# Memory's key rows turned on VectorE and put in place through DRAM, in an attention and gated-FFN kernel

## The chip, the cores and the metric

One Trainium2 chip, one of its cores. The metric is the device time of one execution in microseconds (us). Matmuls run on TensorE (PE in the profile; PEld is its loading of the stationary operand), elementwise work on VectorE (DVE), ScalarE (ACT) and GpSimd (POOL). Transfers are issued by SyncE (SP) and GpSimd and carried out by 16 DMA engines. SBUF is the memory on the chip with 128 partitions, PSUM the eight banks into which TensorE writes, and DRAM the memory off the core.

## The reference

The layer is `x + A(xn) + B(xn)`, with `xn` the normalised `x` of 2048 tokens and D = 448 features. B is a gated FFN. A is attention in four segments of 512 tokens with a memory that is carried from segment to segment; cut to what matters here:

```python
for s in range(4):                       # segments; H = 16 heads of 28
    qs, ks, vs = q[:, :, s], k[:, :, s], v[:, :, s]
    a_dot = softmax(qs @ ks.T * scale + mask) @ vs
    pq = phi(qs)                         # phi(t) = t + 1 if t > 0 else exp(t)
    a_mem = (pq @ M) / (pq @ z + 1e-6)   # the recall
    outs.append(g * a_mem + (1 - g) * a_dot)
    pk = phi(ks)
    M = M + einsum("bhld,bhle->bhde", pk, vs)   # the update
    z = z + pk.sum(tokens)
return concat(outs) @ wo
```

The update sums over tokens, so on TensorE it needs `phi(k)` with the tokens on the partitions. The products of keys and queries have the features there. The rows of `phi(k)` therefore have to be turned.

## The kernel before

The program has two parts. In the **front** (0 to about 140 us) four blocks of 512 tokens pass one after the other; a block is a segment. After it, attention inside the segments, the FFN and the output projection run interleaved, and the change doesn't touch them.

In the front all queues but GpSimd's follow the order in which the code is written. For block `b` it is:

1. `values(b, t)` for the four token tiles t = 0 to 3: 11 matmuls into a PSUM bank `pv` (tag "p", two banks), then a copy by ScalarE into `vst` (`store_values`). After the last tile `vst` goes to DRAM. For b > 1, `recall(b-1)` stands behind tile 3: 16 matmuls of `phi` with the memory state `mst`. For block 0 the value tiles have code of their own ahead of the loop.
2. Seven products `keys_queries(b, c)`, c = 0 to 6, of 128 features each (keys are features 0 to 447, queries 448 to 895): 11 matmuls into `pp`. Even c take a bank of tag "p", odd c one of tag "gu" (two each), so value tiles 0 and 1 of the next block take the banks that products 4 and 6 had. ScalarE and VectorE read `pp` into `qk` and, where needed, into `e`, which is `phi` of the product; the last reader of a bank is VectorE's line 360. `qk` goes to DRAM (`qd`), and the query part of `e` too (`fd`); `phi_queries` reads `fd` back as `phi`, in the layout of the recall, after product 6.
3. Between the products stand: `key_rows` for key chunks 0 to 3, at k = 2 to 5 (TensorE turns four 128x128 pieces of `e` with the identity into a bank `pk`, ScalarE copies that into `kn`); `turn` of the four tiles of the next block's `xn` (`pt`, then `xs`); `normalise` of `xn` for the next block; and in blocks 2 and 3 `divide` and `answer` of the previous block's recall (VectorE's `rc`, GpSimd's scaling of `phi`, VectorE's transpose into `tb`, GpSimd's transfer to `od`).
4. After product 6, for blocks 0 to 2, `update(b)`: 64 small matmuls of `kn` with `vst` into `pmm`, which VectorE adds into `mst`.

VectorE, ScalarE, TensorE and SP each do their instructions in that order; an instruction that waits holds all behind it. SBUF tiles of one name share a fixed number of buffers (`bufs`), and a new tile waits until the one that had its buffer is no longer read.

Of the kernel before, what the change touches and what calls it, by code (L numbers as in the profile page):

```python
# [16 lines left out]
P = 128  # L17
D = 448
# [45 lines left out]
def kernel(  # L64
# [87 lines left out]
    def eight_k(dtype, name):  # L152
        return mid.tile([P, 8, 256], dtype, name=name, tag="8k")
# [128 lines left out]
    with tc.tile_pool(name="front", bufs=2) as sb, tc.manual_schedule(engines=FRONT):  # L282
# [6 lines left out]
        mst = [sb.tile([P, P], F32, name=f"mst{n}", bufs=1) for n in range(2)]  # L289
        one = sb.tile([P, 1], F32, name="one", bufs=1)  # L290
        kn = eight_k(F32, "kn").rearrange("p (t a) n -> p t (a n)", t=NT)

# [48 lines left out]
        def values(b, t):  # L341
            pv = bank("pv", "p")
            value_terms(b, t, pv, TERMS)
            store_values(b, t, pv)

        def keys_queries(b, c):
# [7 lines left out]
            if (c < 4 and b < NB - 1) or (c > 2 and b > 0):  # L354
                e = sb.tile([P, L], F32, name="e", bufs=4)
                A.activation(e, pp, AF.Relu, scale=-1.0)  # L356
                A.activation(e, e, AF.Exp, scale=-1.0)
# [12 lines left out]

        def key_rows(c, e):

            pk = bank("pk", ("m", "pd")[c % 2])
            for t in range(NT):
                T.transpose(pk[:, t * P:(t + 1) * P], e[:, t * P:(t + 1) * P], ident)  # L375
            n = min(P, D - c * P)
            A.activation(kn[:, :, c * P:c * P + n], pk.rearrange("p (t n) -> p t n", t=NT)[:, :, :n], AF.Copy)

# [36 lines left out]
        def answer(b, i, phi):  # L415
            tb = sb.tile([P, L], F32, name="e", bufs=4) if b == NB - 1 else sb.tile([P, L], F32, name="tb", bufs=2)
            V.transpose(tb, phi[:, i])
            nc.gpsimd.dma_start(od[b][P * i:P * (i + 1)], tb)
# [132 lines left out]
        for b in range(NB):  # L551
# [28 lines left out]
            for k, c in enumerate(LAST if last else range(7)):  # L580
                e[c] = keys_queries(b, c)
                if b == 0 and c + 4 < 7:
                    split_qk(c + 4)
                if b > 1:
                    i = k + (1 if last else -1)
                    if 0 < i <= NG:
                        answer(b - 1, i - 1, phi)
                    if 0 <= i < NG:
                        divide(i, phi)
# [13 lines left out]
                if last:  # L603
# [4 lines left out]
                    continue  # L608
                if 2 <= k < 6:
                    key_rows(k - 2, e[k - 2])  # L610
                if k == 6:
                    update(b)
                n = k - 1 if b == 0 else k + 1
# [282 lines left out]
```

## Time and profile before

| | us |
|---|---|
| median of 3 runs (674.81 to 675.7) | 675.15 |
| the profiled execution | 675.51 |
| its span in the profile | 673.7 |
| PE busy in the span | 668.8 |
| DVE busy | 555.1 |
| ACT busy | 341.8 |
| POOL busy | 169.1 |

The profile is of one execution. Its rows give an engine, an operation, tile names as `out<-in`, the count, the busy time and the mean of one in ns, and behind the bar the idle time ahead of them with what ended it. The chain of work that ended last goes back from the last instruction to whatever released each step; TensorE's granted clock is full over the whole span (0.999). `L360` is line 360 of the kernel.

### The profile page before, as it was taken

To read this page: it belongs to the slowest core of one execution; us is meant where nothing else is said; L and a number is where in the kernel's file an instruction comes from. 1 tells how busy PE (TensorE), PEld (TensorE's weight loads), DVE (VectorE), ACT (ScalarE), POOL (GpSimd) and SP (SyncE) were. 2 spreads that over 40 slices of the span, in tenths; PEclk is the share of its full clock that TensorE was granted. 3 is DMA by queue.
4 is the path that set the end of the run, shared out by engine and by line. 5 is a ranking of instruction groups with operands and counts; after the bars stand their busy time and mean duration, and the time that the engine had idled before them with its cause. 6 is when DMAs were issued, how large, how long until landed. Compare 5 with 4: busy or idle time off the path is not lost.

```text
span 673.7 us, 11186 instructions
## 1 busy us (share of the span) xinstructions
PE 668.8 (99%) x3963; PEld 555.5 (82%) x3963; DVE 555.1 (82%) x967; ACT 341.8 (51%) x559; POOL 169.1 (25%) x368
## 2 busy tenths in 40 slices
PE   8999999999999999999999999999999999999998
PEld 8888888878878778787887878787787878778897
DVE  6855584758998989998998899988988898989964
ACT  4947574533646446354554555554554656444320
POOL 4402051305122223122322322222231332221000
PEclk9999999999999999999999999999999999999999
DMA  8536668797123242323243324224342432315272
GB/s 273 189 149 249 226 230 274 268 305 214 41 73 89 71 137 64 102 57 103 70 104 93 85 80 102 61 70 102 88 111 72 85 73 77 65 44 134 68 216 97
DMA packets 46223, 84.42 MB, mean 125 GB/s; under 512 B 6360, under 2 KB 21080, under 8 KB 45656
## 3 DMA queue, kind: packets, MB, share of 16 engines
q1 hardware_dynamic: 43160, 76.37, 37.6%
q0 software_dynamic: 3008, 7.34, 5.3%
q8 instruction: 31, 0.51, 0.3%
q14 instruction: 24, 0.20, 0.1%
HBM read 51.05 MB, written 32.64 MB: 124 GB/s over the span
## 4 chain that ended last, share of the span: by engine, by line
PE 93%; DVE 2%; issue 1%; DMA 1%; ACT 1%; POOL 0%; SPq 0%; POOLq 0%; ACTq 0%
PE pgu L252 40%; PE pd L178 19%; PE pp L351 11%; PE po L829 5%; PE st L665 5%; PE pa L740 5%; PE pv L333 4%; PE pv L489 1%; PE pt L97 1%; DMA wv_raw<-in_w_v 1%; PE pk L375 1%; PE pmm L386 1%; PE n L407 1%; DVE mx L683 0%; DVE w L719 0%
## 5 line engine op out<-in xcount | busy, mean ns | idle before, releaser
L252 PE MATMUL pgu<-xs,wgu 128*128 128x512 f32 x1232 | 315.0, 394 | 0.0
L252 PEld LDWEIGHTS pgu<-xs,wgu 128*128 128x128 f32 x1232 | 226.3, 188 | 44.1 <-issue 2.6
L178 PE MATMUL pd<-wdn,hh 128*128 128x448 f32 x672 | 161.4, 367 | 0.0
L680 POOL TENSOR_SCALAR_AFFINE_SELECT w<-w 128x256 f32<-128x256 f32 (+1 forms) x160 | 80.0, 502 | 236.3 <-ACT w L669 201.9
L178 PEld LDWEIGHTS pd<-wdn,hh 128*128 128x128 f32 x672 | 123.1, 188 | 15.4 <-issue 1.0
L720 ACT ACTIVATE w<-w 128x1024 f32<-128x1024 f32 (+1 forms) x96 | 86.6, 915 | 84.4 <-DVE w L719 83.7
L669 ACT ACTIVATE w<-st 128x512 f32<-128x512 f32 x128 | 75.2, 589 | 49.9 <-PE st L665 46.8
L719 DVE TENSOR_TENSOR w<-w,mb 128x1024 f32<-128x1024 f32 (+1 forms) x96 | 99.6, 1051 | 0.1
L683 DVE TRANSPOSE_TENSOR_REDUCE mx<-w 128x32 f32<-128x1024 f32 x64 | 79.1, 1236 | 13.2 <-POOL w L680 13.0
L351 PE MATMUL pp<-xs,wqk 128*128 128x512 f32 x308 | 75.5, 395 | 0.0
L181 DVE TENSOR_TENSOR acc<-pd,acc 128x448 f32<-128x448 f32 x112 | 67.4, 603 | 1.4 <-PE pd L178 1.4
L351 PEld LDWEIGHTS pp<-xs,wqk 128*128 128x128 f32 x308 | 56.6, 188 | 12.8 <-ACT vst L337 0.8
L665 PE MATMUL st<-qk 84*128 84x128 f32 (+3 forms) x256 | 63.7, 310 | 0.0
L263 ACT ACTIVATE hh<-sg 128x512 fp32r<-128x512 f32 x56 | 35.1, 627 | 47.0 <-DVE sg L262 46.4
L665 PEld LDWEIGHTS st<-qk 84*128 84x128 f32 x256 | 48.4, 189 | 7.7 <-ACT w L669 0.3
L260 ACT ACTIVATE sg<-pgu 128x512 f32<-128x512 f32 x56 | 33.2, 593 | 38.9 <-PE pgu L252 37.7
L709 DVE STREAM_TRANSPOSE mb<-top 128x1024 f32<-128x1024 f32 x32 | 39.7, 1240 | 10.9 <-POOL top L706 10.5
L358 DVE TENSOR_TENSOR qk<-pp,qk 128x512 fp32r<-128x512 f32 x28 | 19.4, 691 | 28.8 <-ACT e L356 19.5
L262 DVE SCALAR_TENSOR_TENSOR sg<-sg,pgu 128x512 f32<-128x512 f32 x56 | 37.3, 665 | 3.7 <-PE pgu L252 3.7
L267 DVE SCALAR_TENSOR_TENSOR hh<-sg,hh 128x512 fp32r<-128x512 f32 x56 | 38.6, 689 | 1.0 <-ACT hh L263 0.6
L740 PE MATMUL pa<-w,vv 128*32 128x128 f32 (+3 forms) x512 | 38.3, 436 | 0.0
L829 PE MATMUL po<-wo,xs 128*128 128x448 f32 (+2 forms) x187 | 36.3, 352 | 0.0
(102 smaller groups left out, 620.9 us busy)
## 6 DMA issues: line engine op xcount, KB each, us to landing
qk<-qd SPq DMA_DIRECT2D x192, 112.0 KB
qd<-qk SPq DMA_DIRECT2D x28, 512.0 KB
raw<-in_w_ffn SPq DMA_DIRECT2D x14, 512.0 KB
vd<-vst SPq DMA_DIRECT2D x4, 1024.0 KB
vv<-vd SPq DMA_DIRECT2D x16, 256.0 KB
od<-w POOLq DMA_DIRECT2D x16, 256.0 KB, 4.1
ob<-od SPq DMA_DIRECT2D x32, 128.0 KB
out<-acc SPq DMA_DIRECT2D x15, 224.0 KB
```

Source lines behind the costliest of these rows:

```text
L178: T.matmul(pd[:, :D], l, r, start=n == 0, stop=n == len(mms) - 1)
L181: V.tensor_add(acc[b][:, t, :], pd[:, :D], acc[b][:, t, :])
L252: T.matmul(dst, wgu[f][:, w, side * P:(side + 1) * P], xs[b][:, a, :], start=n == 0, stop=n == len(TERMS) - 1)
L351: T.matmul(pp, wqk[c][:, w, :], xs[b][:, a, :], start=n == 0, stop=n == len(TERMS) - 1)
L665: T.matmul(st[:, at:at + L - kb * P], self.qk[:KS, 1, h, kb * P:(kb + 1) * P], self.qk[:KS, 0, h, kb * P:], start=True, stop=True)
L669: A.activation(w, st, AF.Copy)
L680: G.affine_select(d, d, pattern=pattern, base=0, channel_multiplier=-1, compare_op=ALU.is_ge, fill=MASK)
L683: V.tensor_reduce(mx[:, 16 * (n - 1):16 * (n + 1)], w3[:, n // 2, :2 * L].rearrange("p (b n) -> p b n", n=32), axis=mybir.AxisListType.X, ...
L719: V.tensor_sub(w, w, m)
L720: A.activation(w, w, AF.Exp, scale=SCALE)
L740: T.matmul(pa[32 * j:32 * j + 32, kb * P:], self.vv[:, kb, 32 * j:32 * j + 32], self.pairs[j // 2].block(j % 2, kb), start=kb == 0, stop=k ...
L829: T.matmul(po[:, cols], xs[b][:, a, t * P:(t + 1) * P], out_weights(w)[:, cols], start=m == 0, stop=m == len(TERMS) - 1)
```

## The change

The key rows no longer pass through TensorE. VectorE turns each 32x32 block of `e` in place of its own grid into a tile `kt` (named `tb`, which now has three buffers in place of two, shared with `answer`). Transfers put the blocks into their places in a new DRAM tensor `kd`, 512 tokens by 448 features: 14 a block, each of 32 x 16 runs of 32 floats. Two more read `kn` back, in runs of 384 and of 64 floats. The update of block b moves behind value tile 2 of block b + 1; since it reads `vst`, the stores of value tiles 0 to 2 of that block move behind it, and tiles 2 and 3 take banks of another tag. `e` has three buffers in place of four.

```diff
+        kd = [dram.tile([L, D], F32, name=f"kd{b}") for b in range(NB - 1)]
...
         def values(b, t):
-            pv = bank("pv", "p")
+            pv = bank("pv", "p" if t < 2 else "gu" if b < NB - 1 else "s")
             value_terms(b, t, pv, TERMS)
-            store_values(b, t, pv)
+            turned.append(pv)
+            if t == 2:
+                update(b - 1)
+            if t > 1:
+                for n in range(len(turned)):
+                    store_values(b, t + 1 - len(turned), turned.pop(0))
+
+        turned = []
...
-                e = sb.tile([P, L], F32, name="e", bufs=4)
+                e = sb.tile([P, L], F32, name="e", bufs=3)
...
-        def key_rows(c, e):
-
-            pk = bank("pk", ("m", "pd")[c % 2])
-            for t in range(NT):
-                T.transpose(pk[:, t * P:(t + 1) * P], e[:, t * P:(t + 1) * P], ident)
+        def turn_keys(b, c, e):
+
             n = min(P, D - c * P)
-            A.activation(kn[:, :, c * P:c * P + n], pk.rearrange("p (t n) -> p t n", t=NT)[:, :, :n], AF.Copy)
+            kt = sb.tile([P, L], F32, name="tb", bufs=3)
+            V.transpose(kt[:n], e[:n])
+            for f in range(0, n, 32):
+                rows = kd[b][:, c * P + f:c * P + f + 32].rearrange("(t r) k -> r t k", r=32)
+                nc.sync.dma_start(rows, kt[f:f + 32].rearrange("r (t k) -> r t k", k=32))
+
+        def key_rows(b, f0, f1):
+
+            nc.sync.dma_start(kn[:, :, f0:f1], kd[b][:, f0:f1].rearrange("(t p) f -> p t f", p=P))
...
-            tb = sb.tile([P, L], F32, name="e", bufs=4) if b == NB - 1 else sb.tile([P, L], F32, name="tb", bufs=2)
+            tb = sb.tile([P, L], F32, name="e", bufs=3) if b == NB - 1 else sb.tile([P, L], F32, name="tb", bufs=3)
...
+                if k < 4 and not last:
+                    turn_keys(b, c, e[k])
...
-                if 2 <= k < 6:
-                    key_rows(k - 2, e[k - 2])
-                if k == 6:
-                    update(b)
+                if k == 3:
+                    key_rows(b, 0, 3 * P)
+                if k == 4:
+                    key_rows(b, 3 * P, D)
```

How the instructions then stand, at three places. First TensorE's queue at the end of block 2 and the start of block 3, before (`pp` are the products, `pk` the turned keys, `pt` the turned `xn`, `pmm` the update, `pv` the values):

```order
L375 MATMUL pk<-ident,e 128x128 x4
L97 MATMUL pt<-ident,xn 128x128 x4
L351 MATMUL pp<-xs_67,wqk_122 128x512 x11
L375 MATMUL pk<-ident,e 128x128 x4
L351 MATMUL pp<-xs_67,wqk_123 128x512 x11
L386 MATMUL pmm<-vst,kn 32x32 x64
L333 MATMUL pv<-wv,xs_68 128x448 x44
```

And after the change:

```order
L97 MATMUL pt<-ident,xn 128x128 x4
L359 MATMUL pp<-xs_67,wqk_122 128x512 x11
L359 MATMUL pp<-xs_67,wqk_123 128x512 x11
L334 MATMUL pv<-wv,xs_68 128x448 x33
L399 MATMUL pmm<-vst,kn 32x32 x64
L334 MATMUL pv<-wv,xs_68 128x448 x11
```

The groups `pk` are gone, and value tiles 0 to 2 now follow product 6 directly, ahead of the update.

Second VectorE's queue in block 2, around product 3, with the semaphores that each row waits for: DMAHW are those of transfers that SP issues, DMASW those that GpSimd issues, one to each in turn. Before, between answer 0 (`tb_1160`) and answer 1 (`tb_1208`):

```order
L417 STREAM_TRANSPOSE tb_1160<-phi_909 128x512 [waits Pool_49]
L131 TENSOR_SCALAR rc_1163<-phi_909 128x16
L132 RECIPROCAL rc_1163<-rc_1163 128x16 [waits DVE_49]
L133 TENSOR_SCALAR rc_1163<-rc_1163,gate_76 128x16 [waits DVE_49]
L105 TENSOR_TENSOR xs3_68<-pt_1174,xs3_68 128x3x128 [waits Activation_49]
L107 TENSOR_TENSOR xs3_68<-pt_1174,xs3_68 64x128
L358 TENSOR_TENSOR qk_1187<-pp_1188,qk_1187 128x512 [waits DMAHW3_49,Activation_49]
L360 SCALAR_TENSOR_TENSOR e_1201<-pp_1188,e_1201 128x512 [waits DMAHW5_49,Activation_49]
L417 STREAM_TRANSPOSE tb_1208<-phi_909 128x512 [waits Pool_49]
```

After, from answer 0 (`tb_1181`) over the keys of product 3 (`tb_1223`) to answer 1 (`tb_1227`), and then the rows around answer 2 (`tb_1265`) and answer 3 (`tb_1302`):

```order
L430 STREAM_TRANSPOSE tb_1181<-phi_912 128x512 [waits DMAHW6_49,DMAHW1_49,DMAHW7_49,DMAHW0_49,Pool_49]
L131 TENSOR_SCALAR rc_1184<-phi_912 128x16
L132 RECIPROCAL rc_1184<-rc_1184 128x16 [waits DVE_49]
L133 TENSOR_SCALAR rc_1184<-rc_1184,gate_76 128x16 [waits DVE_49]
L105 TENSOR_TENSOR xs3_68<-pt_1189,xs3_68 128x3x128 [waits Activation_49]
L107 TENSOR_TENSOR xs3_68<-pt_1189,xs3_68 64x128
L366 TENSOR_TENSOR qk_1202<-pp_1203,qk_1202 128x512 [waits DMAHW3_49,Activation_49]
L368 SCALAR_TENSOR_TENSOR e_1216<-pp_1203,e_1216 128x512 [waits Activation_49]
L383 STREAM_TRANSPOSE tb_1223<-e_1216 64x512 [waits DMASW0_49,DVE_49]
L430 STREAM_TRANSPOSE tb_1227<-phi_912 128x512 [waits DMAHW5_49,DMAHW4_49,DMAHW6_49,DMAHW3_49,Pool_49]
```

```order
L366 TENSOR_TENSOR qk_1244<-pp_1245,qk_1244 128x512 [waits Activation_49]
L368 SCALAR_TENSOR_TENSOR e_1258<-pp_1245,e_1258 128x512 [waits Activation_49]
L430 STREAM_TRANSPOSE tb_1265<-phi_912 128x512 [waits DMASW1_49,Pool_49]
L131 TENSOR_SCALAR rc_1268<-phi_912 128x16
L132 RECIPROCAL rc_1268<-rc_1268 128x16 [waits DVE_49]
L133 TENSOR_SCALAR rc_1268<-rc_1268,gate_76 128x16 [waits DVE_49]
L105 TENSOR_TENSOR xs3_68<-pt_1274,xs3_68 128x3x128 [waits Activation_49]
L107 TENSOR_TENSOR xs3_68<-pt_1274,xs3_68 64x128
L366 TENSOR_TENSOR qk_1282<-pp_1283,qk_1282 128x512 [waits DMAHW2_49,Activation_49]
L368 SCALAR_TENSOR_TENSOR e_1296<-pp_1283,e_1296 128x512 [waits Activation_49]
L430 STREAM_TRANSPOSE tb_1302<-phi_912 128x512 [waits DMASW2_49,Pool_49]
```

The answers are the first transfers that GpSimd issues, so DMASW0, 1 and 2 tell of the landing of answers 0, 1 and 2. Before, answers 0 and 1 wait for no transfer; answer 2 waits for that of answer 0 and answer 3 for that of answer 1.

Third SP's queue in block 2, after the change, from the `qk` of product 2 on:

```order
L372 DMA qd_80<-qk 128x1024
L386 DMA kd_132<-tb 32x16x32 x4
L190 DMA raw<-in_w_ffn 128x1024
L371 DMA fd_84<-e 64x512
L372 DMA qd_80<-qk 128x1024
L386 DMA kd_132<-tb 32x16x32 x2
L390 DMA kn<-kd_132 128x4x384
L371 DMA fd_84<-e 128x512
L372 DMA qd_80<-qk 128x1024
L390 DMA kn<-kd_132 128x4x64
L371 DMA fd_84<-e 128x512 x2
L411 DMA phi<-fd_84 28x4x512 x4
```

Before, the same rows stand there without those of `kd` and `kn`. A read of `kn` waits for the writes of `kd` that it covers, and `fd` and `phi` stand behind it.

## The prediction

> **What bounds the kernel now.** I read the chain of work that ended last first, then the groups of the front stage (0 to 140 us, where all edits lie), then the timelines of single engines.
>
> ```profile
> PE 93%; DVE 2%; issue 1%; DMA 1%; ACT 1%; POOL 0%; SPq 0%; POOLq 0%; ACTq 0%
> L375 PE MATMUL pk<-ident,e 128*128 128x128 f32 x48 | 7.2, 271 | 0.0
> L377 ACT ACTIVATE kn<-pk 128x512 f32<-128x512 f32 (+1 forms) x12 | 6.4, 529 | 0.0
> L337 ACT ACTIVATE vst<-pv 128x448 f32<-128x448 f32 x16 | 8.5, 545 | 12.9 <-PE pv L333 12.3 <-PE pv L489 0.3
> ```
>
> TensorE carries the end: 93% of the chain, no idle of its own before the transposes `pk` (48 of them in 12 groups of four). So every microsecond that TensorE no longer works is won, and every one that it is made to wait is lost. Off the chain, and so worth nothing by themselves, are ScalarE's 12 copies of `pk` into `kn` (6.4 us, gone) and its stores of `vst`, now three at once behind the update: 3 x 0.55 = 1.6 us, while TensorE has the fourth value tile and the recall ahead of the first product that needs a freed bank.
>
> **What is won.** In the chain in order of time (start, length, what), block 1:
>
> ```profile
> 62.35 2.51 PE pp L351 x11
> 65.74 2.51 PE pp L351 x11
> 68.69 2.54 PE pp L351 x11
> ```
>
> From the end of one key/query product to the next start lie 65.74 - 64.86 = 0.88 us with `pt` and `pk` between, and 68.69 - 68.25 = 0.44 us with `pk` alone. So a group of four costs the chain 0.44 us, and 12 groups **5.3 us** (1.76 us a block). The update `pmm` only moves, from ahead of the value tiles to behind the third.
>
> **What VectorE takes on.** Twelve transposes of 128x512, four in each of blocks 0 to 2. Its order makes block 2 the tight one, because there it also turns and stores the answers of block 1:
>
> ```profile
> 92.04 0.69 DVE L358 TENSOR_TENSOR qk<-pp,qk 128x512 fp32r<-128x512 f32 x1 [0.22 <-ACT e L356]
> ...
> 93.31 0.70 DVE L417 STREAM_TRANSPOSE tb<-phi 128x512 f32<-128x512 f32 x1
> 93.94 0.13 DVE L131 TENSOR_SCALAR rc<-phi 128x16 f32<-128x16 f32 x1
> ...
> 96.70 0.70 DVE L417 STREAM_TRANSPOSE tb<-phi 128x512 f32<-128x512 f32 x1
> ...
> 105.18 0.69 DVE L358 TENSOR_TENSOR qk<-pp,qk 128x512 fp32r<-128x512 f32 x1 [1.00 <-ACT e L356]
> 105.84 0.69 DVE L360 SCALAR_TENSOR_TENSOR e<-pp,e 128x512 f32<-128x512 f32 x1
> 106.45 0.28 DVE L391 TENSOR_TENSOR mst<-pmm,mst 128x128 f32<-128x128 f32 x1
> ```
>
> One such transpose holds the queue 0.63 us (93.31 to 93.94). From 92.04 on VectorE has one gap, of 1.00 us, until product 6 is read at 106.45: 14.41 - 1.00 = 13.41 us of work. The transpose of product 0 falls into the idle time ahead of product 1; that of product 1 delays product 2 by 0.63 - 0.22 = 0.41 us, to 92.45. With two more transposes, product 6 is read at 92.45 + 13.41 + 1.26 = **107.1** if nothing new is waited for. The gap is gone, since TensorE comes 1.76 us earlier.
>
> Something new is waited for. The order of VectorE given with the change shows the three `tb` buffers handed on so that the transpose of product 3 takes the buffer of answer 0 and waits for its transfer to land (DMASW0 counts the first transfer that GpSimd issues), answer 2 waits for that of answer 1 (DMASW1) and answer 3 for that of answer 2 (DMASW2). How long a transfer takes is in GpSimd's timeline and, for 86 to 106 us, in the DMA issues; the spread over 86 to 135 us is in the view of the tile:
>
> ```profile
> 97.71 0.59 POOL L418 DMA_DIRECT2D od<-tb  x1 [1.59 <-DVE rc L131]
> od<-tb POOLq DMA_DIRECT2D x4, 256.0 KB, 4.0
> DMA to landing us min/median/max: 2.3/3.7/4.6
> ```
>
> The answer that ends at 96.70 + 0.70 = 97.40 is issued at 97.71, 0.31 us later, and lands 4.0 us after that: 4.31 us. The work that lies between in VectorE's order (three `rc`, two `xs`, two reads of a product) is what now lies between two answers, 96.70 - 94.01 = 2.69 us. So each of the three waits is 4.31 - 2.69 = 1.62 us, 4.9 us in all, and product 6 is read at **112.0**. Behind each waiting transpose stand the reads of the next products, and behind those TensorE:
>
> ```profile
> 104.02 1.23 PE pmm L386 x85
> 105.25 9.01 PE pv L333 x44
> 114.26 1.40 PE n L407 x31
> ```
>
> Product 6 ends at 104.02 now, at 102.26 after. The value tiles of block 3 follow at once, the update no longer between; tile 0 takes the bank of product 4 and tile 1, 9.01 / 4 = 2.25 us later, that of product 6, so at 104.5. It must wait until 112.0: **7.5 us** (the small wait of tile 0 is in it). Bounds: with a landing of 2.3 us (the least in the row) no wait is left and the queue alone costs 107.1 - 104.5 = 2.6 us; with 4.6 us it is 7.5 + 3 x 0.6 = 9.3 us. I take the median of that very stretch.
>
> **Smaller stalls.** In block 0 VectorE is full as well:
>
> ```profile
> 24.00:34.00 10.00, 10.00 (x56) 8.46 (x55) 9.31 (x19) 9.10 (x19) 4.59 (x6) 1.00 0.68 219
> 26.76 2.53 PE pp L351 x11
> 28.49 0.24 POOL L324 COPY xn<-xn 128x64 f32<-128x64 f32 x1 [0.64 <-DVE xn L321]
> 73.06 0.69 DVE L360 SCALAR_TENSOR_TENSOR e<-pp,e 128x512 f32<-128x512 f32 x1
> ```
>
> The first row is a stretch: its length, then busy time of TensorE, of its loads, of VectorE (9.31 of 10 us), ScalarE and GpSimd. Two transposes stand ahead of `xn`, whose last columns GpSimd copies by 28.73 now and by 28.73 + 1.26 = 29.99 then. TensorE turns it after product 3, which ends at 29.29 - 0.44 = 28.85; three quarters of that turn (0.33 us) can go ahead, so it waits 29.99 - 29.18 = **0.8 us**. In block 1 VectorE keeps up, but product 6, which ended at 71.23, was read by 73.75, 2.52 us later, and tile 1 of the next block now comes 2.25 us later: **0.3 us**.
>
> **The transfers.** Each block writes 14 x 512 runs of 128 B to DRAM and reads `kn` back in 512 runs of 1536 and 512 of 256 B. No row shows a 128 B write. The nearest are the 4 B packets of 17.0 to 17.9 us and the 512 B packets of `vv`, 193 to 195 us, both loads:
>
> ```profile
> DMA packets 112, 0.00 MB, mean 0 GB/s; under 512 B 112, under 2 KB 112, under 8 KB 112
> q1 hardware_dynamic: 112, 0.00, 5.7%
> ...
> DMA packets 528, 0.26 MB, mean 131 GB/s; under 512 B 16, under 2 KB 528, under 8 KB 528
> q1 hardware_dynamic: 528, 0.26, 46.2%
> ```
>
> The first is 0.057 x 16 x 0.9 us / 112 = 7 ns a packet, the second 0.462 x 16 x 2 / 528 = 28 ns. A line between them gives 12 ns for 128 B: 448 per engine x 12 = 5.6 us a block, at 28 ns 12.5 us; the read-back, on the same line (70 and 18 ns, 32 each per engine), 2.8 us. A write could also cost more than a load, so neither end is sure; I take 12 ns, the nearer by size. Room for them, by the share of the DMA engines that is busy (last but one number):
>
> ```profile
> 17.00:50.00 33.00, 33.00 (x292) 28.74 (x291) 23.13 (x54) 22.94 (x43) 9.25 (x12) 1.00 0.47 173
> 50.00:82.00 32.00, 32.00 (x305) 27.14 (x312) 17.41 (x37) 21.36 (x38) 4.83 (x6) 1.00 0.65 222
> 55.00:74.00 19.00, 19.00 (x224) 16.09 (x223) 11.84 (x23) 14.00 (x26) 4.21 (x4) 1.00 0.61 223
> 82.00:115.00 33.00, 33.00 (x334) 27.39 (x313) 21.11 (x44) 18.91 (x35) 10.56 (x12) 1.00 0.73 250
> ```
>
> In block 0 half the time is free and nobody waits for `phi`. In block 1 the read of `phi` that the recall (81.4 us) needs is issued from 74.2 us on; before it, 0.39 x 19 - 1.76 = 5.7 us are free against 8.4 us of new work: up to 2.7 us too late, or nothing, if packets overlap as they do elsewhere. I take **1.0 us**. In block 2 TensorE is late by 7.5 us anyway, which covers it; if that cover is gone, the same 1 to 2.7 us come back. SP issues 16 transfers more a block, each for some half a microsecond like `vv`, which has as many runs, and it idles longer than that:
>
> ```profile
> L732 SPq DMA_DIRECT2D vv<-vd x16: 524/530/607, 150.2 to 604.7; - x16
> SPq L364 <- DVE qk L358: 32.7, 12, 4.9
> ```
>
> Its waits for `kd` to land stand ahead of `fd` 4 to 6 and `phi`; at 12 ns they end before `e` 5 is there and cost nothing, at 28 ns they are in the high case. `e` with three buffers instead of four waits for the turned `e` of three products before, or `fd` 3, over 5 us old: nothing.
>
> **The sum.** -5.3 + 7.5 + 0.8 + 0.3 + 1.0 = **+4.3 us**. The profiled execution took 675.5 us, 1.8 us around its span of 673.7; 679.8 for it, and 679.4 beside the median of 675.15, which is 0.4 us lower.
>
> **Rivals.**
> - Landing. If the answers' transfers land within 2.4 us, VectorE never waits and TensorE stalls 2.6 us in block 3; with no lateness of `phi` that is -5.3 + 2.6 + 0.8 + 0.3 = -1.6 us, **673.5**. The sum turns at a landing of 2.6 to 2.9 us. For it: the least was 2.3. Against it: the median of four in that stretch is 4.0, and the new writes share the engines.
> - Price of a write. At 28 ns, block 1 is 12.5 + 2.8 - 5.7 = 9.6 us late, and landings lengthen to the row's 4.6: -5.3 + 9.3 + 0.8 + 0.3 + 9.6 = +14.7, **689.8**. It decides from about 13 ns on.
> - A write that is first read. If each 128 B piece costs a 512 B read and a 512 B write, 56 ns, a block has 25 + 2.8 us of new transfers. Blocks 0 to 2 are busy for 0.47 x 33 + 0.65 x 32 + 0.73 x 33 = 60 us; with 83 more that is 143 us in 93: **+50, about 725**. The Trainium skill, "DMA: Bandwidth & Descriptors", Specifications, says that below 512 B the DMA engines do a read-modify-write. The 4 B packets above cost 7 ns, but they go to SBUF; no row shows such a write to DRAM.
> - The change turning no rows at all on VectorE can be excluded: the 48 transposes are gone from TensorE's order.
>
> **Chances.** Forecast (677 to 684) 0.56; landing short or overlap, 672 to 677, 0.24; price of a write, 684 to 695, 0.14; read first, 0.06. A measurement here tells about 0.2% (1.35 us) from no change. Faster by more: the lower part of the second case, 0.10. Same: the rest of that case, 0.14. Slower: 0.76. The range leaves out some 0.08 at the low end and 0.11 at the high one: 673.5 to 689.
>
> **What would show it.** Three idle times of 1.6 us on VectorE in block 2, put down to `od`, ahead of one `kt` and two `tb`; TensorE's load of `pv` waiting some 7 us for VectorE's read of `e` between blocks 2 and 3; no `pk`, and 0.44 us from product to product where `pt` alone lies between; a short wait at the first `pt` of block 0. If instead `n` waits for `phi`, or `pmm` for `kn`, the price of the writes was wrong; if `pv` waits under 4 us, the landing was.

## Result and the profile after

| | before | after |
|---|---|---|
| median of the runs, us | 674.79 (674.49 to 675.70, 6 runs) | 694.17 (690.35 to 696.08, 6 runs) |
| profiled execution, us | 675.51, span 673.7 | 690.35, span 688.6 |
| packets under 512 B | 6360 | 30168 |

The change makes the kernel slower: ratio 1.0274, 95% interval 1.0243 to 1.0306. The forecast was 679.4 with a range to 689.0. The page of the changed kernel, its slices for TensorE and the granted clock and the shares of the chain of waits:

```profile
PE   8999994999999999999999999999999999999998
PEclk9999998999999999999999999999999999999999
PE 82%; DMA 7%; DVE 6%; issue 2%; ACT 1%; POOL 1%; SPq 0%; DVEq 0%; POOLq 0%; ACTq 0%
```

TensorE has a hole in the seventh slice (103 to 120 us), and in that slice the granted clock is down as well. Its share of the chain fell from 93% to 82%; DMA and VectorE took 10 of these 11 points.

The timeline of TensorE shows where each stage begins (start, length, what; in brackets the idle time before it and what ended it). Before, the first product of each block and the first scores:

```profile
18.67 7.65 PE L351 MATMUL pp<-xs,wqk 128*128 128x512 f32 x33
49.91 5.20 PE L351 MATMUL pp<-xs,wqk 128*128 128x512 f32 x22
82.58 5.31 PE L351 MATMUL pp<-xs,wqk 128*128 128x512 f32 x22
115.60 5.29 PE L351 MATMUL pp<-xs,wqk 128*128 128x512 f32 x22
151.25 0.40 PE L665 MATMUL st<-qk 84*128 84x512 f32 x1
```

The same view of the changed kernel, with the waits:

```profile
17.99 10.16 PE L359 MATMUL pp<-xs,wqk 128*128 128x512 f32 x44
46.51 0.98 PE L399 MATMUL pmm<-vst,kn 128*32 128x32 f32 x90 [1.33 <-DMA kn<-kd]
49.74 5.20 PE L359 MATMUL pp<-xs,wqk 128*128 128x512 f32 x22
72.56 4.68 PE L334 MATMUL pv<-wv,xs 128*128 128x448 f32 x22 [0.97 <-DVE e L368]
80.81 2.87 PE L420 MATMUL n<-phi,mst 28*32 28x512 f32 x6
84.91 5.33 PE L359 MATMUL pp<-xs,wqk 128*128 128x512 f32 x22
106.08 2.48 PE L334 MATMUL pv<-wv,xs 128*128 128x448 f32 x11 [1.00 <-DVE e L368]
116.46 6.58 PE L334 MATMUL pv<-wv,xs 128*128 128x448 f32 x22 [7.89 <-DVE e L368]
127.68 5.28 PE L359 MATMUL pp<-xs,wqk 128*128 128x512 f32 x22
163.34 0.40 PE L680 MATMUL st<-qk 84*128 84x512 f32 x1
174.28 1.48 PE L178 MATMUL pd<-wdn,hh 128*128 128x448 f32 x6 [1.32 <-DVE acc L181]
```

From these starts the 14.9 us of span fall into stages:

| stage | before | after | difference | what is seen in it |
|---|---|---|---|---|
| to the first product | 18.67 | 17.99 | -0.68 | ahead of all edits; 17.96 in e9, which has the same start as before |
| block 0 to block 1 | 31.24 | 31.75 | +0.51 | -1.76 saved; 0.32 for `xn`, 1.33 for `kn` |
| block 1 to block 2 | 32.67 | 35.17 | +2.50 | -1.76; 0.97 for `e`; the recall takes 4.10 us, not 1.17 |
| block 2 to block 3 | 33.02 | 42.77 | +9.75 | -1.76; 8.89 for `e`; two value tiles take 6.58 us, not 4.68 |
| block 3 to the first scores | 35.65 | 35.66 | 0.0 | |
| the rest | 522.45 | 525.26 | +2.81 | 1.32 for `acc` and smaller waits |

Behind the long wait stand three waits of VectorE, and a fourth one comes at 171 us. VectorE's timeline of the changed kernel:

```profile
102.03 0.70 DVE L383 STREAM_TRANSPOSE tb<-e 64x512 f32<-64x512 f32 x1 [1.43 <-DMA od<-tb]
107.67 0.71 DVE L430 STREAM_TRANSPOSE tb<-phi 128x512 f32<-128x512 f32 x1 [1.64 <-DMA od<-tb]
114.52 0.71 DVE L430 STREAM_TRANSPOSE tb<-phi 128x512 f32<-128x512 f32 x1 [3.43 <-DMA od<-tb]
171.21 0.71 DVE L430 STREAM_TRANSPOSE e<-phi 128x512 f32<-128x512 f32 x1 [2.86 <-DMA od<-e]
```

The first three are the ones forecast, in the order forecast. The transfers that they wait for took 3.7, 3.9 and 5.7 us from issue to landing, where 4.0 was taken for each, so the first two waits are close to the 1.62 us worked out and the third is twice as long. The fourth was not forecast: the four answers of the last block go round three `e` buffers, where they had four, so the last one waits for the first one's transfer.

The two value tiles that took 6.58 us ran at half clock. The stretches of the changed kernel (length; busy time of TensorE, its loads, VectorE, ScalarE, GpSimd; then granted clock, DMA share, GB/s):

```profile
112.00:114.00 2.00, 0.00 (x0) 0.00 (x0) 0.00 (x0) 0.00 (x0) 0.00 (x0) 0.94 0.90 326
114.00:116.00 2.00, 0.00 (x0) 0.00 (x0) 1.48 (x3) 0.00 (x0) 0.47 (x1) 0.50 0.11 38
120.00:122.00 2.00, 2.00 (x10) 1.87 (x9) 0.00 (x0) 0.00 (x0) 0.00 (x0) 0.85 1.03 209
```

The clock falls some 5 us after TensorE stopped and comes back 6.8 us later.

### The profile page after: what moved, and what is told of

The parts are those of the page before. It is cut to its first block, busy times and chain, and to the rows that moved or that the text cites. A ratio compares the mean times of both kernels' runs of the same rounds, so it can differ in the third digit from the quotient of the medians.

```text
span 688.6 us, 11163 instructions
## 1 busy us (share of the span) xinstructions
PE 669.9 (97%) x3915; PEld 551.1 (80%) x3915; DVE 561.5 (82%) x979; ACT 335.0 (49%) x547; POOL 169.8 (25%) x368
## 2 busy tenths in 40 slices
DMA packets 71567, 89.93 MB, mean 131 GB/s; under 512 B 30168, under 2 KB 46424, under 8 KB 71000
## 4 chain that ended last, share of the span: by engine, by line
PE 82%; DMA 7%; DVE 6%; issue 2%; ACT 1%; POOL 1%; SPq 0%; DVEq 0%; POOLq 0%; ACTq 0%
PE pgu L252 38%; PE pd L178 19%; PE pa L755 5%; PE st L680 5%; PE po L844 5%; PE pp L359 5%; DMA kd<-tb 2%; PE pv L334 2%; DMA fd<-e 2%; DMA od<-tb 1%; PE pv L502 1%; DVE e L368 1%; DVE qk L366 1%; DMA kn<-kd 1%; DMA phi<-fd 1%
## 5 line engine op out<-in xcount | busy, mean ns | idle before, releaser
L334 PE MATMUL pv<-wv,xs 128*128 128x448 f32 x132 | 30.4, 385 | 9.9 <-DVE e L368 9.9
```

## Experiments

All times are medians; the ratio is to the kernel before, timed beside each. e6, e9 and e12 to e16 are edits of the kernel before, the others of the changed kernel.

| run | median, us | ratio, 95% interval |
|---|---|---|
| e1 own buffers for the turned keys | 687.94 | 1.0205, 1.0183 to 1.0226 |
| e2 other banks for value tiles | 692.52 | 1.0263, 1.0248 to 1.0278 |
| e3 fourth answer in a `tb` | 689.09 | 1.0206, 1.0191 to 1.0221 |
| e4 wait filled with 52 products | 693.59 | 1.0284, 1.0261 to 1.0307 |
| e5 no transfers of the keys | 677.14 | 1.0034, 1.0021 to 1.0047 |
| e6 moved update alone | 679.57 | 1.0065, 1.0044 to 1.0086 |
| e7 e1, e2 and e3 together | 684.49 | 1.0142, 1.0123 to 1.0161 |
| e8 wait filled with 30 products | 694.38 | 1.0267, 1.0229 to 1.0304 |
| e9 update moved, but early | 676.17 | 1.0014, 1.0004 to 1.0023 |
| e10 e7 without the transfers | 674.88 | 0.9988, 0.9975 to 1.0001 |
| e11 transfers straight into `kn` | 756.19 | 1.1198, 1.1181 to 1.1214 |
| e12 change in block 0 alone | 677.75 | 1.0043, 1.0025 to 1.0060 |
| e13 the same, turned earlier | 675.81 | 1.0008, 0.9999 to 1.0017 |
| e14 three groups of block 0 | 675.75 | 1.0008, 1.0000 to 1.0017 |
| e15 before, without the transposes | 671.16 | 0.9944, 0.9931 to 0.9958 |
| e16 the same in block 0 alone | 673.87 | 0.9988, 0.9980 to 0.9997 |

**e1, own buffers.**

```diff
-            kt = sb.tile([P, L], F32, name="tb", bufs=3)
+            kt = two_k("kt") if b == 2 else sb.tile([P, L], F32, name="tb", bufs=3)
```

> In block 2 the turned keys get two buffers of their own (of the store that the feed-forward part uses later), so that the answers alone share the three `tb`; everything else as in the changed kernel. Buffer theory (the stall between blocks 2 and 3 is made by VectorE's waits for `od` to land, because keys and answers pass three buffers round): the waits of 1.43, 1.64 and 3.43 us ahead of `kt` 3 and of answers 2 and 3 go, VectorE reads product 6 some 6.5 us earlier, and TensorE's wait ahead of value tiles 0 and 1 of block 3 falls from 8.9 to about 2.4 us (the queue alone); with the low clock behind it (2.1 us) gone as well, 8 us less than the 694.2 of the changed kernel: 684 to 688. Rival, price of the transfers: the transposes now wait for the `kd` writes of two products before instead, or the queue alone keeps TensorE: under 3 us less, 691 to 694, and the idle time of VectorE is put down to `kd`.

6.2 us less than the changed kernel. VectorE waits for no `od` in block 2, and TensorE's timeline has:

```profile
110.23 6.28 PE L334 MATMUL pv<-wv,xs 128*128 128x448 f32 x22 [2.51 <-DVE e L368]
```

The wait of 8.9 us is 2.51 us, what VectorE's queue alone was forecast to cost (2.6). But 2.5 us still bring the half clock (6.28 us for the two tiles), and the recall now waits 1.07 us for `phi`, which the long wait had covered. The buffer theory holds for the wait: the key transfers are all still there, and the answers of block 2 take 3.2 to 6.4 us to land, but nobody waits for them any more. Part of what this frees goes to the next wait.

**e2, other banks.**

```diff
-            pv = bank("pv", "p" if t < 2 else "gu" if b < NB - 1 else "s")
+            pv = bank("pv", "s" if t < 2 else "p")
```

> Value tiles 0 and 1 of blocks 1 to 3 take the two banks of the turned rows `pt`, which are long read by then, and tiles 2 and 3 those of products 4 and 6; VectorE's order and its waits stay. Bank theory (TensorE stalls only because tile 1 takes the bank of product 6 while VectorE is late): tiles 0 and 1 start at once (9.9 us of wait in blocks 2 and 3 go), tile 2 of block 3 waits for product 4 (some 1.6 us) and tile 3 for product 6 (some 1.8 us): 3.4 us instead of 9.9, so 6.5 us less, and up to 2 us more if the clock stays full: 685.5 to 688. Rival (VectorE's lateness reaches TensorE all the same, by the update or the first products of the next block): the wait is as long at tile 3 or at the next product, 692 to 694.

```profile
111.83 6.24 PE L334 MATMUL pv<-wv,xs 128*128 128x448 f32 x22 [2.80 <-DVE xs L107]
```

Only 1.7 us less. The premise was wrong: VectorE is so late that even `pt` is not yet read (the wait is for `xs`). The wait shrinks to 2.80 us, but others appear, each with half clock behind it: 1.80 us for `kn`, and 2.05 us for `phi` at 122 us. The rival, that the lateness reaches TensorE by other ways, is nearer.

**e3, the fourth answer.**

```diff
-            tb = sb.tile([P, L], F32, name="e", bufs=3) if b == NB - 1 else ...
+            tb = sb.tile([P, L], F32, name="e", bufs=3) if b == NB - 1 and i < 3 else ...
```

> The last of the four answers of block 3 takes a `tb` buffer instead of the first of the three `e` buffers. Theory (with three `e` instead of four, that transpose waits for the first answer's transfer to land, 2.86 us at 168.4 us, and VectorE then reads the feed-forward banks and the scores late): that wait goes, TensorE's waits of 1.3 and 0.2 us at 173 and 187 us go, and the part behind block 2, 2.8 us longer than before, is as long as before: 2.8 us less, 690 to 692.5 beside 694.2. Rival (the part behind block 2 is longer for another reason, such as the transfers put off into it): no change, 693.5 to 695.

```profile
129.79 5.28 PE L359 MATMUL pp<-xs,wqk 128*128 128x512 f32 x22
```

With a span of 687.9, block 3 and all that follows take 558.1 us, as in the kernel before (673.7 - 115.60); in the changed kernel it is 560.9. So the 2.8 us at the end are this buffer. The median falls by 5.1 us, more than that; in e4 below the same wait is 2.10 us long and half clock follows it, which would make up much of the difference in runs that have no trace.

**e4 and e8, the wait filled.**

```diff
+            if b == NB - 1 and t == 1:
+                cold = bank("cold", "pd")
+                for _ in range(52):   # e8: 30
+                    T.matmul(cold[:, :P], ident, ident, start=True, stop=True)
             value_terms(b, t, pv, TERMS)
```

> 52 products of the identity with itself (about 6.9 us at 0.13 us each) stand between value tiles 0 and 1 of block 3, where TensorE waits 7.9 us; nothing reads what they write. Clock theory (the granted clock falls because TensorE stands still, to 0.50 and 0.74 in the 6 us behind the wait, which costs 2.1 us there, and more in the runs with a mean clock of 0.987 to 0.990): the clock stays at 1.00, the two tiles behind take 4.5 us instead of 6.6, the mean clock is 0.998 or 0.999 in all runs, and the time falls by 2 us against 690.35 and by up to 6 us against the median of 694.2: 687 to 691, with runs within 1 us of each other. Rival (the clock falls for another reason, such as the transfers at the same time): the clock falls all the same and the time stays at 690 to 696.

```profile
108.53 11.77 PE L347 MATMUL cold<-ident 128*128 128x128 f32 x104
120.06 4.67 PE L334 MATMUL pv<-wv,xs 128*128 128x448 f32 x22
176.74 2.18 PE L178 MATMUL pd<-wdn,hh 128*128 128x448 f32 x6 [2.10 <-DVE acc L181]
```

The clock stayed at 1.00 and the two tiles took 4.67 us, so the half clock does come from TensorE standing still. No time was won, since the filler was 4 us too long: a product, which the trace counts as two, takes 0.226 us, and the 0.13 in the expectation was one of its halves. At 176.74 us it shows the same thing from the other side: a wait of 2.10 us for `acc`, and half clock behind it.

> As with 52 products of the identity, but 30: one takes 0.226 us, not the 0.13 that the beginning of the kernel showed, so that 52 took 11.8 us where 7.9 were idle, and 30 take 6.8. Clock theory: TensorE stands still for 1 us or less, the clock stays at 1.00 and the two value tiles behind take 4.7 us, not 6.6: 2 us less than the changed kernel, 691 to 692.5 by the median and 688 to 689 if no other wait brings the half clock. Rival (what the filler saves is lost at the next wait): the recall or the update waits longer, 693.5 to 695.

```profile
118.84 4.68 PE L334 MATMUL pv<-wv,xs 128*128 128x448 f32 x22 [1.74 <-DVE e L372]
```

At its own place the filler did what was expected (4.68 us behind a wait of 1.74). The time did not fall: the recall of block 1 and the wait for `acc` brought the half clock instead. The median misses its expectation; the mechanism holds.

**e5, no transfers.**

```diff
-            for f in range(0, n, 32): ...
-                nc.sync.dma_start(rows, kt[f:f + 32].rearrange("r (t k) -> r t k", k=32))
-            nc.sync.dma_start(kn[:, :, f0:f1], kd[b][:, f0:f1].rearrange("(t p) f -> p t f", p=P))
-        G.memset(kn[:, :, D:], 0.0)
+        G.memset(kn[:, :, :], 0.0)
```

> The changed kernel without the transfers of the turned keys: `kd` is neither written nor read, and `kn` is set to zero once (the memory's update then adds zeros); the transposes on VectorE, their buffers and the order of TensorE stay. Theory (the transfers cost time of their own, by the time that they take from the DMA engines): the update's wait of 1.3 us for `kn` in block 0 goes, the recall of block 2 (4.1 us instead of 1.2, waiting for `phi`) starts without a wait, and the transfers of answers land in 3.8 to 4.0 us instead of up to 5.8, which takes some 1.8 us from the wait between blocks 2 and 3; with that wait still some 7 us, the half clock behind it and the 2.8 us at the end stay: 6 us less than the changed kernel, 686 to 689. Rival (the transfers are hidden, and `phi` is late because VectorE and SP are): only the wait for `kn` goes, 692 to 694.

17.0 of the 19.4 us are gone, far more than either theory said. TensorE, VectorE and GpSimd of e5:

```profile
104.81 6.00 PE L334 MATMUL pv<-wv,xs 128*128 128x448 f32 x22 [2.51 <-DVE e L368]
```

```profile
95.65 0.70 DVE L383 STREAM_TRANSPOSE tb<-e 64x512 f32<-64x512 f32 x1
```

```profile
93.23 0.80 POOL L428 DMA_DIRECT2D od<-tb  x1 [1.53 <-DVE rc L131]
```

But e5 takes away more than the transfers. The last row is the issue of answer 0, which lands 3.4 us later, at 96.7. In the changed kernel the turned keys of product 3 wait for that landing; here they begin at 95.65, ahead of it. None of the eight transposes into `tb` in block 2 of e5 waits for the transfer of an answer. The reading that fits is that keys which no transfer reads give their buffer back as soon as they are written, so that the answers have the three buffers to themselves. So e5 shows what the transfers and the buffers that they hold cost together. That the shared buffers are needed for VectorE's three waits is shown by e1; what the transfers cost without them is the difference of e7 and e10 below.

**e6 and e9, the moved update alone.** The kernel before, keys turned by TensorE, with the new `values` of the change; in e9 the update stands behind value tile 0.

```diff
             turned.append(pv)
-            if t == 2:
+            if t == 0:   # e9
                 update(b - 1)
```

> The kernel before with the one part of the change that moves the update behind the third value tile and the stores behind it, with the value tiles' banks as in the change; the keys are still turned by TensorE, and buffers stay as before. Theory (the moved update costs only what value tile 1 waits for the reading of product 6): product 6 is read 2.5 to 2.6 us after its end and tile 1 comes 2.25 us after it, 0.3 us in each of blocks 2 and 3, no half clock behind so short a wait: 675 to 676.5. Rival (the stores put together behind the update come too late for the banks, or for the transfer of `vd`): 677 to 680, with idle time of TensorE put down to ScalarE's `vst`.

4.4 us more than before, where 0.3 a block was expected. The wait for `e` is indeed 0.36 us; the rest stands in the recall of block 2. TensorE's timeline, and the DMA rows of e6 for 115.3 to 115.5 us:

```profile
114.97 1.09 PE L414 MATMUL n<-phi,mst 28*32 28x512 f32 x16
117.89 1.76 PE L414 MATMUL n<-phi,mst 28*32 28x512 f32 x16 [1.83 <-issue]
119.58 6.21 PE L358 MATMUL pp<-xs,wqk 128*128 128x512 f32 x22
```

```profile
q8 instruction: 1, 0.02, 30.3%
```

TensorE stops in the middle of the recall with nothing in the trace to wait for ("issue"), behind a 16 KB packet of an instruction queue, and the half clock follows (6.21 us for two products, not 5.3). The order alone doesn't bring the stop: in block 1 of e6, and in block 2 of e5 (behind a wait of 2.51 us), the same update, value tile and recall stand one behind the other, and the recall runs through in 1.14 us.

> As the kernel with the moved update alone (679.6), but the update stands behind the first value tile instead of the third; the stores stay together behind the third. Theory (the moved update costs what TensorE waits for its own instructions: update and recall are 384 short ones with one value tile between, TensorE stands still for 1.8 us in the middle of the recall of block 2 with nothing to wait for in the trace, just behind a 16 KB packet of the instruction queue, and the half clock follows): with three value tiles (6.7 us) between them the fetch is in time, 675 to 676.8. Rival (the late stores or the banks of the value tiles cost it): 678.5 to 681, as before.

676.17, as the theory said (1.2 us above before are left); the recall of block 2 runs through:

```profile
113.78 1.74 PE L414 MATMUL n<-phi,mst 28*32 28x512 f32 x32
```

So what costs in block 2 is the update close ahead of the recall (together 160 short matmuls in the trace, not the 384 of the expectation), not the late stores or the banks, which e9 has too. That TensorE waits for its instructions there is argued from the packet's time; no run takes the fetch away by itself.

**e7, three edits undone.**

> The three edits together: the keys' own two buffers in block 2, the banks of `pt` for value tiles 0 and 1, and the fourth answer of the last block in a `tb`. Theory A (the waits add up): from 687.9 with own buffers alone go 2.8 us at the end, 2.5 us between blocks 2 and 3, 0.8 between 1 and 2 and some 1.8 of half clock: 679 to 681. Theory B (behind them the chain of `fd` written, landed and read as `phi` is the bound of blocks 1 and 2, lengthened by the transfers): TensorE only waits longer at the recall, which starts no earlier than `phi` lands, some 10 to 13 us after product 6 is read; only the 2.8 us at the end are won, 683.5 to 686, with waits of 2 to 5 us ahead of the recall.

```profile
115.97 1.49 PE L399 MATMUL pmm<-vst,kn 128*32 128x32 f32 x90 [3.69 <-DMA kn<-kd]
```

By its time theory B, and the waits do not add up. In block 1 the recall is as long as in the changed kernel (4.05 us), as theory B has it. In block 2 TensorE reaches the update earlier, and the wait stands there, for `kn`, and not ahead of the recall.

**e10, the same without transfers.** The edits of e7 and e5 together.

> The three edits (own buffers in block 2, banks of `pt`, fourth answer in a `tb`) together with the transfers of the keys left out (`kd` not written or read, `kn` zero, so the memory stays zero): what the change could give at most. Theory (the parts add up: 677.1 without transfers, less 2.8 us at the end and the half clock behind it, less 2.5 and 1.4 between blocks 2 and 3, less 0.4 between 1 and 2): 669 to 671.5. Rival (with nothing else to wait for, TensorE waits for its instructions at the recall, as in the kernel with the moved update alone, 3.5 us): 672.5 to 675.

```profile
112.07 2.74 PE L417 MATMUL n<-phi,mst 28*32 28x512 f32 x28 [1.66 <-DMA phi<-fd]
114.74 7.08 PE L359 MATMUL pp<-xs,wqk 128*128 128x512 f32 x22
```

Not 669 to 671.5 but the time of before. It lies in the rival's range, but not by the rival's mechanism: the recall waits for `phi`, not for instructions. TensorE is ready 4.8 us earlier, at 109.4 us instead of 114.2; VectorE has read product 6 only 2.7 us earlier, at 103.9 instead of 106.5, and `fd` and `phi` take 8 us from there (the chain of e10 has 2.22 and 5.90). That is the profiled execution, the longest of nine, with half clock behind the wait (7.08 us for two products). Four of the nine had a mean clock of 0.999 or 1.000 and took 672.71 to 673.94 us; the five with 0.995 to 0.997 took 674.88 to 676.97. So where the half clock stays away, some 1.7 us of the 5.3 may be won (673.3 is the mean of the four, 674.97 the kernel before); those four have no trace.

e7 and e10 differ in the transfers alone, and VectorE waits for no answer in block 2 of either. So the transfers by themselves cost 9.4 us: e7 is 9.33 us above the kernel before timed beside it, e10 0.09 under. They also make others land later. From issue to landing, the four answers of block 2 in e7, then in e10 (the view of tile `od`, 84 to 115 us):

```profile
DMA to landing us min/median/max: 3.0/5.9/9.0
DMA to landing us min/median/max: 2.4/3.5/4.0
```

**e11, straight into `kn`.**

```diff
+            for j in range(4):
+                for f in range(0, n, 32):
+                    nc.sync.dma_start(kn[32 * j:32 * j + 32, :, c * P + f:c * P + f + 32],
+                                      kt[f:f + 32].rearrange("r (t j k) -> j r t k", j=4, k=32)[j])
```

> The three edits together, and the turned keys go by transfer straight from SBUF to their place in `kn` (56 transfers a block of 128 pieces of 128 B, four for each 32 features, since a transfer here has three dimensions), not through DRAM and back. Theory (the cost is the time on the DMA engines and two landings one behind the other): 5.5 us of packets a block instead of some 9, no wait for `kn`, `phi` at most 1 to 2 us late: from 684.5 to 676 to 681. Rival (SP issues 56 transfers a block at 0.5 us, 28 us of the 33 us of a block, and `fd` and `phi` stand behind them): the recalls wait for `phi` longer than 3 us, 686 to 700.

```profile
L386 SPq DMA_DIRECT2D kn<-tb x112: 585/599/1478, 24.7 to 118.7; - x112
```

The rival, and worse than it said: 56 issues a block at 0.6 us (duration least/median/most, ns) are 33.6 us of SP's queue, as long as a block, and everything behind them is late.

**e12 to e14, block 0 alone.** The kernel before, with only block 0 turned by VectorE; e13 turns right behind the reading of `e`, e14 leaves product 3 with TensorE.

```diff
-            pv = bank("pv", "p")
+            pv = bank("pv", ("s", "s", "pd", "p")[t] if b == 1 else "p")
...
+            if b == 1 and t < 3:
+                return
+            if b == 1:
+                update(0)
...
+                if b == 0 and k < 4:   # e14: 3
+                    turn_keys(k, e[k])
```

> The kernel before, with the change in block 0 alone, where VectorE has no answers to turn and no recall follows: VectorE turns the four `e` (behind the normalising of the next block's tile, into the store of `phi`, which is free until block 1 ends), the transfers go through DRAM as in the change, and the update of block 0 stands behind all four value tiles of block 1, whose banks are those of `pt`, `pd` and product 4. Blocks 1 and 2 are as before: keys turned by TensorE, update at the end of the block. Theory (what the change saves is real where no wait takes its place): four groups less, 1.76 us, and no wait for `kn`, which landed at 46.4 us in the changed kernel, where TensorE comes to the update at about 46.9: 673 to 674, a ratio of 0.997 to 0.9985. Rival (the update waits for `kn`, or the transfers make the loads of block 1 late): 675 to 677.

`kn` landed at 50.3, not 46.4: TensorE waits 1.90 and 1.11 us for its two parts, and the half clock follows, as the rival said. The profiled execution (681.52 us) is one of the longest of twelve, 675.4 to 681.87.

> As the change in block 0 alone, but each `e` is turned as soon as it is read, ahead of the normalising, as in the change. Theory (the saving is real where no wait takes its place): `kn` lands at some 46.4 us as in the changed kernel, TensorE comes to the update behind value tile 3 at about 46.7, so it waits 0.5 us at most; 1.76 us saved, 0.3 lost at the first `pt`: 673.3 to 674.3, ratio 0.9975 to 0.999. Rival (the transfers of the keys fill SP's queue and the DMA engines, so that `kn` lands at 49 us or later whatever the order): a wait of over 1.7 us with the half clock behind it, 676 to 678.5.

```profile
113.93 5.30 PE L359 MATMUL pp<-xs,wqk 128*128 128x512 f32 x22
150.17 0.47 PE L690 MATMUL st<-qk 84*128 84x512 f32 x1 [0.43 <-DVE rc L133]
174.08 0.50 PE L690 MATMUL st<-qk 84*128 84x384 f32 x2 [1.07 <-ACT w L694]
```

> As e13, but only products 0 to 2 of block 0 are turned by VectorE and go through DRAM (12 transfers and one read); the half group of product 3 stays on TensorE, with ScalarE's copy. Theory: the read of `kn` no longer waits for the transfers of product 3, so it lands at 43 us or earlier and the update waits for nothing; three groups are saved, 1.3 us, and 0.2 to 0.3 are lost at a `pt`: 673.7 to 674.5, ratio 0.998 to 0.9995. Rival (a saving on TensorE in block 0 is lost again behind it, at the recall's `phi` or the loads of the feed-forward part): 674.8 to 676, with a wait of TensorE for `phi` or `qk` that the kernel before does not have.

In e13 the update waits for nothing, and from the first product (18.47) TensorE needs 95.46 us to block 3 where it needed 96.93: 1.47 us less, as worked out. Yet the kernel is not faster: the scores then wait for VectorE's `rc` and ScalarE's `w`, waits that the kernel before does not have. e14 gives the same time (675.75), with a wait of 1.14 us at the same scores. Neither expectation held; the rival of e14 was right about the loss, not about its place.

**e15 and e16, transposes only taken away.** The kernel before without `key_rows`, in e16 for block 0 alone.

```diff
-                if 2 <= k < 6:
+                if b > 0 and 2 <= k < 6:   # e16; e15: never
                     key_rows(k - 2, e[k - 2])
```

> The kernel before with the 12 groups of transposes and ScalarE's copies left out and nothing in their place (`kn` is set to zero once, so the memory stays zero); update, order and buffers as before. Theory A (each microsecond taken from TensorE in the front stage is won): 5.3 us less than 675.1, 669.5 to 670.5, and block 3 begins some 5.3 us earlier after its first product. Theory B (behind the front other things end last: the recall's `phi`, which has under 1 us of slack, and VectorE and ScalarE in the first units of attention): 672 to 675, with waits of TensorE for `phi` at the recalls or for `w` and `rc` at the first scores that the kernel before does not have.

> The same for block 0 alone (blocks 1 and 2 turn their keys on TensorE as before; `kn` is zero in block 0, so the first block is missing from the memory). Theory A: 1.76 us less, 673.0 to 673.8, so that what e13 lost comes from its added transfers and transposes. Theory B (the later stages swallow it, whatever was added): 674.4 to 675.8, with block 3 begun 1.7 us earlier after the first product and waits at the first scores as in e13.

```profile
17.99 10.19 PE L351 MATMUL pp<-xs,wqk 128*128 128x512 f32 x44
109.98 5.29 PE L351 MATMUL pp<-xs,wqk 128*128 128x512 f32 x22
```

In the profiled execution of e15 TensorE needs 91.99 us from the first product to block 3 where it needed 96.93, 4.9 us less, and the first scores come 35.66 us later, as before, with no wait of TensorE. That is nearly theory A. The span is 5.5 us shorter, but 0.68 of that lies ahead of the first product, where nothing was edited. By the medians 3.7 of 5.3 us are won in e15 and 1.0 of 1.76 in e16, between the two theories. In the trace of e16 block 0 is 1.6 us shorter, and 0.7 us come back in block 1, whose recall takes 1.92 us instead of 1.17. So most of what is taken off TensorE reaches the end, and what e13 lost was given back by what it adds. Why that shows only at the scores, 100 us behind the last added transfer, stays open.

## Why the prediction was right and wrong

The direction was right, and the forecast lay 14.8 us under the median (10.6 in the profiled executions). Of these 10.6 us the traces place 9.3: 1.9 at `phi` in block 1, 1.3 at `kn` in block 0, 1.4 in VectorE's part, 2.8 at the `e` buffers and 1.9 in the half clock. By its steps:

- **The price of a write** (12 ns, between 7 and 28) was right. The DMA rows of the changed kernel for 58.0 to 58.6 us, where nearly all packets are those of `kd`:

```profile
DMA packets 606, 0.08 MB, mean 126 GB/s; under 512 B 606, under 2 KB 606, under 8 KB 606
q1 hardware_dynamic: 606, 0.08, 73.8%
```

  0.738 x 16 x 0.6 us / 606 = 11.7 ns. Over the whole trace the 21504 packets of 128 B took 12.2 ns in the mean. The rival of a write that is first read, at 56 ns, is refuted here.
- **The engines' time** was right too. The shares of the three blocks are

```profile
18.00:50.00 32.00, 30.35 (x268) 25.61 (x267) 22.72 (x54) 19.10 (x34) 8.70 (x12) 1.00 0.76 236
50.00:85.00 35.00, 33.77 (x298) 25.64 (x296) 19.91 (x41) 19.67 (x36) 4.83 (x6) 1.00 0.86 266
85.00:128.00 43.00, 33.83 (x298) 27.10 (x299) 23.99 (x48) 16.89 (x30) 10.47 (x12) 0.92 0.78 234
```

  so 24 + 30 + 34 = 88 us against the 60 of before: 28 more, where 3 x 8.4 = 25 were forecast.
- **The step that failed is what that time does to others.** It stood in the sum as 1.0 us, the lateness of `phi` in block 1. With the shared buffers out of the way the transfers cost 9.4 us (e7 and e10). In the profiled execution of the changed kernel these parts of it can be seen: 2.9 us at `phi` in block 1; 1.33 us at `kn` in block 0, where the room on the engines was taken for cover; and the third answer that VectorE waits for, which lands after 5.7 us where 4.0 was taken. The landing is not a constant: with the transfers the answers of block 2 take up to 9.0 us (e7), without them up to 4.0 (e10). That they land later because the small packets stand ahead of them on the same engines is the reading that fits, and was not tried by itself.
- **VectorE's part** (+7.5 us) was right in its mechanism and nearly in size: 8.9 us, nearly all at tile 1 and from the waits named. Own buffers take the three waits away (e1). Its queue alone costs 2.51 us (e1, e5) where 2.6 was worked out.
- **The smaller stalls**: 0.32 us for 0.8 at `xn`; 0.97 for 0.3 at tile 1 of block 2, 0.36 without transfers (e5).
- **"`e` with three buffers instead of four: nothing"** failed too. The step looked at the products and forgot that `answer` names the same tile in the last block, behind the front, where no edit was thought to lie: 2.8 us of the profiled time, 5.1 by the median of e3.
- **The half clock** was no term at all. It costs 1.9 us in the profiled execution. The other five runs of the changed kernel had a mean clock of 0.987 to 0.993 against its 0.994 and took up to 5.7 us longer; that more of its waits brought the half clock there, as in e3 and e8 at the recall of block 1, fits, but those runs have no trace.
- **"The update only moves"** was wrong by itself (4.4 us, e6). In the changed kernel that stop does not show; TensorE stands still longer ahead of it, but no run shows that this is why.
- **-5.3 us**, by the rule that every microsecond which TensorE no longer works is won, was nearly right: 4.9 us in the profiled execution of e15, 3.7 by the medians, with nothing put in the place of the transposes. What is put there took it back even without the transfers: with those and the shared buffers out of the way (e10) the change gives 0.9988 (0.9975 to 1.0001), no difference that can be told. In its profiled execution the recall waits for `phi`, and `phi` follows VectorE, which with its added transposes keeps only part of TensorE's lead.

Of the rivals, the one on the price of a write gave 689.8, nearest to the time, by the wrong cause: a write cost 12 ns, not 28. The short landing did not come: the three that VectorE waited for took 3.7 to 5.7 us.

## What to carry to other kernels

Work taken off the engine that carries the chain is won only as far as what ends just behind it has slack: here the recall's `phi`, which VectorE's new work and the transfers made later at the same time. A transfer's price is paid by the others that the DMA engines carry at the same time, so ask of each new transfer who is landing beside it and with how much slack. When buffers of a tile are taken away, follow every place that names it, in all blocks.

## What the runs showed of the hardware

**A short stop costs half the clock afterwards.** In e1 TensorE stands still for 2.51 us and starts again at 110.2; only then the clock falls. The stretches of e1:

```profile
110.00:112.00 2.00, 1.77 (x7) 1.65 (x8) 1.30 (x2) 0.00 (x0) 0.00 (x0) 0.84 0.97 360
112.00:114.00 2.00, 2.00 (x7) 1.75 (x7) 0.00 (x0) 0.00 (x0) 0.00 (x0) 0.50 1.08 399
114.00:116.00 2.00, 2.00 (x10) 1.83 (x9) 0.00 (x0) 0.00 (x0) 0.00 (x0) 0.81 1.02 385
```

At 0.50 it stays for 0.16 x 2 / 0.5 + 2.0 + 0.19 x 2 / 0.5 = 3.4 us, which costs 1.7 us. The clock records of the traces give the same 3.4 us for e2, e5 and e6, and 6.8 us, twice as long, for the changed kernel (behind 7.9 us), e7 and e10. Waits of 1.33 us (`kn`), 1.74 us (e8) and 1.96 us (e5) were followed by full clock, while 1.73 and 1.80 us in e2, 1.83 in e6 and 2.10 in e4 (the `pd` behind it took 2.18 us, not 1.48) brought the half clock: from 1.7 to 2 us the length alone does not decide. In the recall of block 1 four short matmuls and a wait of 1.3 us were followed by half clock too (e3, e8). The Trainium skill, "TensorE: Matmul & The Clock Gate", HAM oscillation, warns of gaps over some 3.4 us; here half of that was enough, and the length of the slow stretch agrees with that window.

**An update next to the recall.** In block 2 of e6 the update and the recall (128 and 32 short matmuls as the trace counts), with one value tile between them, were followed by a stop of TensorE of 1.83 us with nothing to wait for; with three value tiles between them it was gone (e9). In block 1 of e6 the same order brought no stop, so the program order does not tell it.
